# Attention and two feed-forward layers on one core: another list schedule behind the same instructions

## The chip, the core and the metric

The kernel runs on one core of a Trainium2 chip. Its time is device microseconds for one execution, and the smaller the better. The core's engines are named as in the profile: PE multiplies matrices, PEld loads its weights, DVE and POOL work on vectors, ACT evaluates functions, SP issues the transfers. Each engine takes its instructions in the order in which they were written into its own stream and waits on semaphores for the others.

## What is computed

```
scores = scale * q @ k.T                       # batch 4, 8 heads, 576 positions, 64 wide
masks  = local (0 <= i-j < 32) for heads 0..3, strided (i-j >= 0, same rest mod 32) for 4..7
x      = softmax(where(masks, scores, -1e9)) @ v      # -> 2304 tokens x 512
h  = x @ w_in                                  # 512 -> 2048
g  = (a0 + a1 h + a2 h^2 + a3 h^3) / (1 + |b0||h| + |b1|h^2 + 1e-6)
y  = g @ w_out                                 # 2048 -> 512
h  = y @ w_in2                                 # 512 -> 1024
s  = h * softmax(h)
out = ((s - mean) / sqrt(var + 1e-6) * g_ln) @ w_out2 # 1024 -> 512
```

## The kernel before

All large products are made of three float16 matmuls (high by high, high by low, low by high); attention stays in float32. Batch 0's attention is done first, in 12 units of one pair of heads and up to two key blocks each (`attn_scores2` ... `attn_xlo`). Of each unit PE makes the scores, DVE their maxima, ACT the exponentials, DVE the sums and reciprocals, POOL the normalised weights, PE their transposes (`MATMUL bank<-ident,p`), ACT copies these out (`q<-bank`), PE multiplies with v (`bank<-q,vl` or `bank<-q,vs`), and ACT and DVE write the high and low halves of x (`xs<-bank`). Beside it DVE converts the weights: `w_conv` puts a word together from two halves in three instructions of 128x1024 each (writing into tiles called `T`, `gtb`, or free places in `wi_h`, `wo_h`, `wo_l`, `ysb`), and `w_split` makes a high half on ACT and a low half on DVE (`wi_l<-...`).

Then 72 groups follow, 9 blocks of 256 tokens by 8 groups of 256 features. A group is 24 matmuls into one of two banks (`mm_h`, `bank<-xs,wi_h` and `wi_l`), an elementwise chain over ACT, POOL and DVE that ends with `q<-q,bank`, `bank<-q,bank` and `p<-p,ac,bank` on DVE and frees the bank, two halves of the result in a ring (`gtb`, or free weight places for the first 16 groups), and 24 more matmuls (`mm_y`, `banks<-gtb,wo_h`). Group n+2 needs the bank of group n. Below, "group n" counts from 0, and "the end of group n" is its last DVE instruction. Beside the groups run the attention of batches 1 to 3 on spare slots, the conversion of `w_out`, `w_in2` and `w_out2` (`w2_split` runs on POOL for its low halves, `wo_l<-ws,wo_h`), and the second layer, 18 tiles of 128 tokens (`mm_in2`: `banks<-wi_h,ysb`; a softmax and a norm on ACT and DVE in `ws`; transposes by DMA; `mm_out2`: `bank<-wo_h,T`).

What sets the order is the class `Order`. The program is recorded, not emitted. `record` (L156) notes each instruction's reads, writes and predecessors; `cost` (L201) gives each a planned duration; `run` (L237) makes a list schedule over all engines; `emit` (L334) writes the instructions out in that order, so that nearly every row of the profile bears line L341 and tiles must tell them apart. `run` first goes backwards once and gives every instruction a due time, then places them forward: on each engine, among those that can begin within `SLACK` (L110) of the earliest, the one with the earliest due time. A reader on another engine may begin after the writer's end, the writer's delay and a margin:

```
LAG = dict(PE=0.25, ACT=0.15, DVE=0.13, POOL=0.1, SP=0.0)
EARLY, PEARLY = 0.3, 1.5
o.ready = max(o.ready, end + (0.0 if o.eng == op.eng == "PE" else 0.06 if o.eng == op.eng
          else LAG[op.eng] + (PEARLY if o.eng == "PE" else EARLY)))
```

A matmul's planned duration is doubled while a count of recent matmul time (`heat`, `warm`, L307) is low, whatever the matmuls' type. Instructions marked `op.port` (POOL, and DVE instructions with two operands in SBUF or in its fast forms) are planned one after the other (`port`).

Of the kernel before, what the change touches and what calls it, by code (L numbers as in the profile page):

```python
# [106 lines left out]


BUSY = 1e9
SLACK = 0.2  # L110
RATE = 330e3


class Order:
# [86 lines left out]
    def cost(self, op):  # L201
        def size(x):
            n = 1
            for d in x.shape[1:]:
                n *= d
            return n

        ins = [(b, x) for b, x in op.ins if size(x) > 1]
        psum = any(b for b, _ in op.ins + op.outs)
        out = (op.outs or op.ins)[0][1]  # L210
        n = max([size(out)] + [size(x) for _, x in ins])
        op.port, op.land = False, 0.0
        if op.eng == "PE":
            f32 = op.ins[-1][1].dtype == F32
            op.t = max(0.03, size(out) / 2400 * ((3.6 if op.call == "transpose" or out.shape[0] > 64 else 1.8) if f32 else 1))
        elif op.eng == "ACT":
            op.t = 0.08 + n * 0.00088 + (0.05 if psum else 0) + (0.09 if "accum_out" in op.k else 0)
            op.t += 0.08 if n > 300 and hasattr(op.k.get("bias"), "shape") else 0
        elif op.eng == "DVE":
            sb = [x for b, x in ins if not b]  # L220
            two = op.call in ("scalar_tensor_tensor", "tensor_tensor")
            fast = not two and not psum and op.call == "tensor_scalar"
            op.t = 0.07 + n / (1900 if fast else 960) + (0.08 if "accum_out" in op.k else 0)
            op.t += 0.06 * sum(1 for b, x in op.ins if size(x) == 1)
            op.port = n >= 8 and (len(sb) >= 2 if two else fast)
        elif op.eng == "POOL":
            two = op.call == "tensor_tensor"
            h = two and out.dtype == F16
            op.t = 0.1 + n * (0.002 if h else 0.0022 if two else 0.00125 if op.call == "tensor_scalar" else 0.001)
            op.t += 0.1 if op.call == "tensor_scalar" and n < 32 else 0  # L230
            op.port = bool(ins)
        else:
            op.t = 0.06
            b = n * self.SIZE[out.dtype] * out.shape[0]
            op.land = b

    def run(self):  # L237
        ops = self.ops
        LAG = dict(PE=0.25, ACT=0.15, DVE=0.13, POOL=0.1, SP=0.0)
        EARLY, PEARLY = 0.3, 1.5  # L240

        after = 0.0
        for i, op in enumerate(ops):
            op.then = list(op.post)
            for v in op.values:
                v.__dict__.setdefault("users", []).append(i)
        for q in self.queues.values():
            for v, w in zip(q, q[len(q[0].homes):]):
                for j in v.users:
                    if j < w.users[0]:  # L250
                        ops[j].then.append(w.users[0])
        for op in reversed(ops):
            x = min([ops[j].due - (LAG[op.eng] + EARLY if ops[j].eng != op.eng else 0.0) for j in op.then], default=0.0)
            if op.eng == "PE":
                x = min(x, after)
            d = op.t
            if op.eng == "SP":
                d = 2.0 + op.land / 330e3
            op.due = x - d
            if op.eng == "PE":  # L260
                after = op.due
        free = {e: 0.0 for e in self.real}
        cells, port, dma = {}, 0.0, 0.0
        avail = {e: [] for e in self.real}
        need = [len(op.pre) for op in ops]
        for i, op in enumerate(ops):
            op.ready = 0.0
            if not need[i]:
                avail[op.eng].append(i)

        def begin(op):
            x = max(free[op.eng], op.ready)
            if op.port:
                x = max(x, port)
            for v in op.values:
                if v.home is None:
                    f = [max(cells.get(c, 0.0) for c in h) for h, _ in v.homes]
                    x = max(x, min(f)) if v.queue[0] is v else BUSY
            return x

        done, seq, heat, warm = 0, [], 0.0, False
        while done < len(ops):
            best = None
            for e, xs in avail.items():
                if not xs:
                    continue
                c = [(begin(ops[i]), ops[i].due, i) for i in xs]
                t = min(c)[0]
                if t == BUSY:
                    continue  # L290
                t, d, i = min((x for x in c if x[0] <= t + SLACK), key=lambda x: x[1:])
                if best is None or t < best[0]:
                    best = (t, i)
            assert best is not None, "no instruction can be placed"
            t, i = best
            op = ops[i]
            avail[op.eng].remove(i)
            for v in op.values:
                if v.home is None:
                    f = [(max(cells.get(c, 0.0) for c in h), j) for j, (h, _) in enumerate(v.homes)]  # L300
                    v.home = min(f)[1]
                    v.queue.pop(0)
                    for c in v.homes[v.home][0]:
                        cells[c] = BUSY
            d = op.t
            if op.eng == "PE":
                heat = min(3.4, max(0.0, heat - max(0.0, t - free["PE"])) + d)  # L307
                warm = heat > 3.3 or warm and heat > 1.5
                d = d if warm else 2 * d
            end = t + d  # L310
            free[op.eng] = end
            if op.port:
                port = end
            if op.eng == "SP":
                dma = max(dma, t + 0.5) + op.land / RATE
                end = dma + 1.6
            op.end = end
            for v in op.values:
                v.left -= 1
                v.end = max(getattr(v, "end", 0.0), end)  # L320
                if not v.left:
                    for c in v.homes[v.home][0]:
                        cells[c] = v.end + LAG[op.eng] + EARLY
            for j in op.post:
                o = ops[j]
                o.ready = max(o.ready, end + (0.0 if o.eng == op.eng == "PE" else 0.06 if o.eng == op.eng else LAG[op.eng] + (PEARLY if o.eng == "PE" else EARLY)))
                need[j] -= 1
                if not need[j]:
                    avail[o.eng].append(j)
            seq.append((t, i))  # L330
            done += 1
        return seq

    def emit(self, seq):  # L334
        def real(x):
# [994 lines left out]
```

## Time and profile before

| | |
|---|---|
| three runs | 770.37, 772.98, 773.19 us; median 772.98 |
| profiled execution | 773.43 us, of which the span from first to last instruction is 771.6 |
| PE busy | 712.6 us (92%), 5406 instructions |
| DVE busy | 592.0 us (77%), 1194 instructions |
| ACT, POOL busy | 481.8 us (62%), 328.6 us (43%) |
| mean granted clock of PE | 0.929 of full |
| chain that ended last | PE 71%, DVE 17%, DMA 4%, issue 4%, ACT 3% |

The profile's page gives one profiled execution. A view by stretches gives each engine's busy time and the granted clock; the timeline gives single instructions with the idle time before them and what ended it. Where PE is busy for the whole of a stretch at full clock, only fewer matmuls could shorten it; where it is not, the difference is what an order of instructions can win or lose.

### The profile page before, as it was taken

How to read it: one execution, taken by the hardware profiler on the slowest of the kernel's cores; microseconds unless marked ns; L12 is line 12 of the kernel's file. 1: busy time of each engine (PE TensorE's matmuls, PEld its weight loads, DVE VectorE, ACT ScalarE, POOL GpSimd, SP SyncE). 2: the span in 40 equal slices, each digit the busy share in tenths (PEclk: the TensorE clock that was granted, in tenths of full speed). 3: DMA queues.
4: the chain of work that ended last, by engine and by line, in shares of the span. 5: the costliest groups of instructions: out<-in, count | busy, mean ns of one | idle time of the engine just before them, and what ended most of it. 6: DMA issues, size and time to landing. Idle time of an engine off the chain costs nothing.

```text
span 771.6 us, 14358 instructions
## 1 busy us (share of the span) xinstructions
PE 712.6 (92%) x5406; PEld 540.0 (70%) x5406; DVE 592.0 (77%) x1194; ACT 481.8 (62%) x1143; POOL 328.6 (43%) x312
## 2 busy tenths in 40 slices
PE   3985667999998998999999999999999999999996
PEld 3863456888887887787777777777777777765442
DVE  6789999989999999798976677666666766744562
ACT  2685568678778867977766676455555646533342
POOL 3322234664667948465353435344444535320000
PEclk9555567999999999999999999999999999999999
DMA  9988701124414221123121020102201011012134
GB/s 272 320 209 218 197 1 33 34 97 142 123 57 140 60 70 34 34 63 61 28 47 42 2 42 1 42 1 43 42 1 42 10 33 42 1 42 55 41 82 96
DMA packets 68101, 55.98 MB, mean 73 GB/s; under 512 B 39616, under 2 KB 56000, under 8 KB 67520
## 3 DMA queue, kind: packets, MB, share of 16 engines
q1 hardware_dynamic: 68032, 55.07, 27.6%
q8 instruction: 42, 0.69, 0.4%
q14 instruction: 27, 0.22, 0.1%
HBM read 40.90 MB, written 4.72 MB: 59 GB/s over the span
## 4 chain that ended last, share of the span: by engine, by line
PE 71%; DVE 17%; DMA 4%; issue 4%; ACT 3%; SPq 0%; POOL 0%; ACTq 0%; DVEq 0%
PE bank L341 39%; PE banks L341 32%; DVE p L341 3%; DVE tiny L341 3%; DMA qkb<-in_qk_dram 2%; DVE T L341 2%; DVE gtb L341 2%; DMA vs<-in_v_dram 1%; DVE ws L341 1%; DVE bank L341 1%; DVE xs L341 1%; DVE q L341 1%; DVE wi_l L341 1%; ACT p L341 1%; DVE ysb L341 1%
## 5 line engine op out<-in xcount | busy, mean ns | idle before, releaser
L341 PE MATMUL bank<-xs,wi_h 128*128 128x256 f16 x1152 | 203.5, 281 | 13.4 <-DVE p L341 9.4
L341 PE MATMUL bank<-xs,wi_l 128*128 128x256 f16 x576 | 161.5, 280 | 2.3 <-DVE wi_l L341 2.3
L341 PE MATMUL banks<-gtb,wo_h 128*128 128x256 f16 x896 | 152.1, 273 | 0.1
L341 POOL TENSOR_SCALAR q<-A,aba 128x512 f32<-128x512 f32 x72 | 65.0, 902 | 181.4 <-ACT A L341 181.3
L341 PEld LDWEIGHTS <-wi_h 128*128 128x128 f16 x1152 | 115.7, 101 | 29.6 <-issue 13.4
L341 PEld LDWEIGHTS <-wo_h 128*128 128x128 f16 x1152 | 112.4, 98 | 21.9 <-issue 0.8
L341 PE MATMUL banks<-gtb,wo_l 128*128 128x256 f16 x448 | 122.0, 273 | 0.0
L341 DVE SCALAR_TENSOR_TENSOR p<-p,ac,bank 128x512 f32<-128x512 f32 x144 | 107.5, 747 | 4.7
L341 ACT ACTIVATE A<-bank,ih 128x512 f32<-128x512 f32 x72 | 49.4, 686 | 79.4 <-PE bank L341 79.1
L341 POOL TENSOR_TENSOR q<-q,A 128x512 f32<-128x512 f32 x72 | 91.6, 1272 | 5.5
L341 PE MATMUL banks<-wi_h,ysb 128*128 128x512 f16 x288 | 91.1, 379 | 0.0
L341 PE MATMUL bank<-wo_h,T 128*128 128x512 f16 x272 | 86.3, 383 | 3.0 <-DMA T<-ws 3.0
L341 DVE TENSOR_TENSOR p<-p,bank 128x512 f32<-128x512 f32 x72 | 49.1, 682 | 50.2 <-ACT p L341 49.7
L341 POOL TENSOR_TENSOR gtb<-p,gtb 128x512 f16<-128x512 f32 x56 | 73.5, 1315 | 25.2 <-ACT gtb L341 25.0
L341 PEld LDWEIGHTS <-T 128*128 128x128 f16 x408 | 40.1, 99 | 47.7 <-DMA T<-ws 4.0
L341 PEld LDWEIGHTS <-ysb 128*128 128x128 f16 x432 | 42.2, 98 | 44.0
L341 DVE SCALAR_TENSOR_TENSOR q<-q,bank 128x512 f32<-128x512 f32 x72 | 49.1, 682 | 24.6 <-ACT bank L341 18.7
L341 PEld LDWEIGHTS <-wi_l 128*128 128x128 f16 x576 | 58.1, 101 | 12.3 <-DVE wi_l L341 2.4
L341 POOL TENSOR_TENSOR e<-e,tiny 96x508 f32<-96x508 f32 (+3 forms) x36 | 35.6, 989 | 72.1 <-DVE tiny L341 32.3
L341 ACT ACTIVATE L<-q 128x512 f32<-128x512 f32 x72 | 45.3, 629 | 26.1 <-POOL q L341 26.1
L341 PEld LDWEIGHTS <-wo_l 128*128 128x128 f16 x576 | 56.5, 98 | 6.4
L341 ACT ACTIVATE e<-bank,tiny 96x127 f32<-96x127 f32 (+2 forms) x132 | 45.8, 356 | 20.4 <-DVE tiny L341 15.9
(257 smaller groups left out, 1435.2 us busy)
## 6 DMA issues: line engine op xcount, KB each, us to landing
qkb<-in_qk_dram SPq DMA_DIRECT2D x28, 304.0 KB, 4.5
out_dram<-ot SPq DMA_DIRECT2D x18, 256.0 KB, 2.4
wo_h<-in_w_out_dram SPq DMA_DIRECT2D x4, 1024.0 KB, 6.2
wo_l<-in_w_out_dram SPq DMA_DIRECT2D x4, 1024.0 KB, 7.1
vl<-in_v_dram SPq DMA_DIRECT2D x4, 768.0 KB, 4.2
wi_h<-in_w_in_dram SPq DMA_DIRECT2D x3, 1024.0 KB, 5.0
wi_l<-in_w_in_dram SPq DMA_DIRECT2D x3, 1024.0 KB, 5.6
wo_h<-in_w_in_dram SPq DMA_DIRECT2D x3, 1024.0 KB, 16.6
```

Of the source, the lines that this page charges most:

```text
L341: getattr(self.real[op.eng], op.call)(*[real(x) for x in op.a], **{k: real(x) for k, x in op.k.items()})
```

## The change

Only the planner is changed; every recorded instruction stays, and the number on each engine is the same (DVE 1176, PE 5039 matmuls, ACT 907, POOL 315). The planned durations of matmuls, small ACT instructions and transfers are set anew; a reader's margin falls from 0.3 to 0.1 and for PE from 1.5 to 0.5; a follower on the same engine now waits for the engine's delay (0.06 before); `SLACK` falls from 0.2 to 0.05. A forward placement is followed by a backward one from the planned end, which gives new due times, in four turns, and the order with the earliest planned end is kept.

```diff
-SLACK = 0.2
-RATE = 330e3
@@ cost
         if op.eng == "PE":
             f32 = op.ins[-1][1].dtype == F32
-            op.t = max(0.03, size(out) / 2400 * ((3.6 if op.call == "transpose" or out.shape[0] > 64 else 1.8) if f32 else 1))
+            op.t = size(out) / 2400 + 0.0025
+            if op.call == "transpose":
+                op.t = 2 * op.t
+            elif f32:
+                op.t = 2 * size(out) / 2400 + 0.055 if out.shape[0] == 64 else 4 * op.t + 0.03
...
+            op.t = max(op.t, 0.11)
...
+    LAG = dict(PE=0.21, ACT=0.14, DVE=0.12, POOL=0.09, SP=0.0)
+    EARLY, PEARLY, SLACK = 0.1, 0.5, 0.05
+
+    def lag(self, op, to, early=1.0):
+        if op.eng == to.eng:
+            return 0.0 if op.eng == "PE" else self.LAG[op.eng]
+        return self.LAG[op.eng] + (0.07 if to.eng == "POOL" else 0.0) + early * (self.PEARLY if to.eng == "PE" else self.EARLY)
@@ run
-        LAG = dict(PE=0.25, ACT=0.15, DVE=0.13, POOL=0.1, SP=0.0)
-        EARLY, PEARLY = 0.3, 1.5
...
+        self.first_due()
+        best = None
+        for k in range(self.TURNS):
+            seq, end, homes = self.forward()
+            if best is None or end < best[0]:
+                best = (end, seq, homes)
+            if k < self.TURNS - 1:
+                self.backward(end)
...
+    TURNS = 4
...
+    def backward(self, T):
...
+        for _ in ops:
+            best = None
+            for e, xs in avail.items():
+                if xs:
+                    c = [(max(free[e], ops[i].ready, port if ops[i].port else 0.0), -ops[i].end, -i) for i in xs]
+                    t = min(c)[0]
+                    t, d, i = min((x for x in c if x[0] <= t + self.SLACK), key=lambda x: x[1:])
+                    if best is None or t < best[0]:
+                        best = (t, -i)
...
+            op.due = -end
+            for j in op.before:
+                o = ops[j]
+                o.ready = max(o.ready, end + self.lag(o, op, 0.5))
...
@@ forward (the second half of run before)
-                o.ready = max(o.ready, end + (0.0 if o.eng == op.eng == "PE" else 0.06 if o.eng == op.eng else LAG[op.eng] + (PEARLY if o.eng == "PE" else EARLY)))
+                o.ready = max(o.ready, end + self.lag(op, o))
```

Three places of the order follow. The first is DVE in batch 0's attention, at the low half of x of unit 6 (`xs_107` and `xs_108`, 128x8x14); the tiles `wo_l`, `wo_h` and `wi_l` beside it belong to the conversion of `w_in`. Before:

```order
L341 TENSOR_SCALAR wo_l<-wo_l 128x1024
L341 SCALAR_TENSOR_TENSOR wo_l<-wo_l 128x1024 x2
L341 TENSOR_REDUCE tiny<-bank_87 108x2
L341 SCALAR_TENSOR_TENSOR wi_l<-wo_h,scl_wi,wi_h 128x4x256
L341 TENSOR_REDUCE tiny<-smb_129 126x4
L341 RECIPROCAL tiny<-tiny 126x4
L341 SCALAR_TENSOR_TENSOR wi_l<-T_102,scl_wi,wi_h 128x4x256
L341 SCALAR_TENSOR_TENSOR xs_107<-bank_88,xsc_134,xs_107 128x8x14
L341 SCALAR_TENSOR_TENSOR xs_108<-bank_88,xsc_134,xs_108 128x8x14
```

With the change:

```order
L409 TENSOR_REDUCE tiny<-g_t 128x1
L409 TENSOR_SCALAR wo_h<-wo_l 128x1024
L409 TENSOR_REDUCE tiny<-bank_86 108x2
L409 SCALAR_TENSOR_TENSOR xs_107<-bank_88,xsc_134,xs_107 128x8x14
L409 SCALAR_TENSOR_TENSOR xs_108<-bank_88,xsc_134,xs_108 128x8x14
L409 SCALAR_TENSOR_TENSOR wo_h<-wo_l,wo_h 128x1024
L409 TENSOR_REDUCE tiny<-bank_87 108x2
L409 SCALAR_TENSOR_TENSOR wo_h<-wo_l,wo_h 128x1024
```

Eight instructions that stood ahead of the low half of unit 6 now stand behind it: two `wo_h<-wo_l,wo_h`, the three of `wo_l<-wo_l`, the two `wi_l` and one maximum.

The second place is POOL where it makes the low halves of the last weight, `wo_l<-ws`, between the groups' own instructions (`q`, `gtb`) and the normalisation of batch 2's attention (`e`). Before:

```order
L341 TENSOR_TENSOR q_97<-q_97,A_99 128x512
L341 TENSOR_TENSOR gtb<-p_94,gtb 128x2x256
L341 TENSOR_TENSOR e_92<-e_92,tiny 108x2x108
L341 TENSOR_TENSOR wo_l<-ws_104,wo_h 128x512 x4
L341 TENSOR_SCALAR q_98<-A_99,aba 128x512
L341 TENSOR_TENSOR q_98<-q_98,A_99 128x512
```

With the change:

```order
L409 TENSOR_TENSOR gtb<-p_96,gtb 128x2x256
L409 TENSOR_TENSOR wo_l<-ws_104,wo_h 128x512 x2
L409 TENSOR_SCALAR q_98<-A_99,aba 128x512
L409 TENSOR_TENSOR q_98<-q_98,A_99 128x512
L409 TENSOR_TENSOR e_92<-e_92,tiny 108x2x108
L409 TENSOR_TENSOR wo_l<-ws_104,wo_h 128x512 x2
L409 TENSOR_TENSOR gtb<-p_94,gtb 128x2x256
```

The four in a row are now two pairs. On DVE, the two small instructions `ac_154<-ih_152,tiny` that stood before the `q` of group 26 now stand before that of group 23, three groups ahead of these pairs.

The third place is DVE between the `q` of group 19 and that of group 20 (`q_98` and `q_97` here); `ws_104` and `T_102` belong to the conversion of `w_out2`. Before:

```order
L341 SCALAR_TENSOR_TENSOR q_98<-q_98,bank_87 128x512
L341 SCALAR_TENSOR_TENSOR bank_87<-q_98,bank_87 128x512
L341 SCALAR_TENSOR_TENSOR p_95<-p_95,ac_144,bank_87 128x512
L341 TENSOR_REDUCE tiny<-bank_89 96x2
L341 SCALAR_TENSOR_TENSOR xs_107<-bank_88,xsc_151,xs_107 128x128
L341 SCALAR_TENSOR_TENSOR xs_108<-bank_88,xsc_151,xs_108 128x64
L341 TENSOR_REDUCE tiny<-bank_89 96x2
L341 SCALAR_TENSOR_TENSOR T_102<-wo_l,T_102 128x1024
L341 SCALAR_TENSOR_TENSOR q_97<-q_97,bank_86 128x512
```

With the change:

```order
L409 SCALAR_TENSOR_TENSOR q_98<-q_98,bank_87 128x512
L409 SCALAR_TENSOR_TENSOR bank_87<-q_98,bank_87 128x512
L409 SCALAR_TENSOR_TENSOR p_95<-p_95,ac_144,bank_87 128x512
L409 TENSOR_REDUCE tiny<-smb_129 96x4
L409 RECIPROCAL tiny<-tiny 96x4
L409 SCALAR_TENSOR_TENSOR xs_108<-bank_88,xsc_151,xs_108 128x192
L409 TENSOR_SCALAR ws_104<-wo_h 128x1024
L409 TENSOR_SCALAR qkb_127<-qkb_127 128x576
L409 SCALAR_TENSOR_TENSOR ws_104<-wo_h,ws_104 128x1024
L409 SCALAR_TENSOR_TENSOR q_97<-q_97,bank_86 128x512
```

By the `q` of group 20 five more instructions have been issued than before: the second `T<-wo_l,T`, `ws<-wo_h`, `ws<-wo_h,ws`, one `qkb<-qkb` and the `xs` of 128x192. On PE, by the first `mm_h` matmul of group 22, ten 512-wide matmuls of the second layer's tile 0 (`banks<-wi_h,ysb` and `wi_l`) and four transposes of attention have been issued more. From group 30 on the groups' matmuls stand at the same place on PE.

## Rows read from the trace of the kernel before

**Rows 1.** Busy time by stretches: us, PE, PEld, DVE, ACT, POOL busy (instructions), clock, DMA, GB/s.
```profile
20.00:60.00 40.00, 34.74 (x187) 30.12 (x188) 33.69 (x71) 30.10 (x104) 11.12 (x9) 0.50 0.90 248
60.00:130.00 70.00, 43.02 (x238) 31.75 (x238) 68.36 (x138) 43.76 (x105) 22.73 (x15) 0.56 0.48 124
130.00:207.00 77.00, 76.12 (x720) 66.35 (x719) 71.81 (x157) 58.91 (x163) 45.59 (x46) 1.00 0.29 90
207.00:264.00 57.00, 52.82 (x482) 44.96 (x482) 54.53 (x113) 45.44 (x115) 41.21 (x35) 1.00 0.28 90
264.00:298.00 34.00, 33.49 (x304) 28.70 (x301) 32.78 (x54) 23.90 (x56) 21.36 (x23) 1.00 0.17 55
298.00:321.00 23.00, 20.89 (x170) 16.15 (x168) 20.80 (x44) 18.65 (x58) 14.27 (x15) 0.93 0.12 29
321.00:747.00 426.00, 425.74 (x3202) 307.89 (x3200) 288.81 (x579) 247.71 (x520) 165.56 (x150) 1.00 0.17 35
747.00:772.00 25.00, 17.98 (x76) 7.34 (x74) 8.75 (x19) 7.47 (x14) 0.00 (x0) 0.93 0.34 84
```

**Rows 2.** Timeline near 300 us: start, duration, engine, instruction [idle before, releaser].
```profile
300.10 5.40 DVE L341 TENSOR_SCALAR ac<-ih,tiny 128x8 f32<-128x8 f32 x2
300.22 4.50 POOL L341 TENSOR_TENSOR wo_l<-ws,wo_h 128x512 f16<-128x512 f32 x4
...
307.65 0.38 PE L341 MATMUL bank<-xs,wi_h 128*128 128x256 f16 x2 [1.77 <-DVE p L341]
```

**Rows 3.** Timeline of DVE, a small fast instruction with no POOL run beside it.
```profile
294.60 0.36 DVE L341 TENSOR_SCALAR ac<-tiny 128x8 f32<-128x8 f32 x2
```

**Rows 4.** Timeline of DVE near 260 us: what now stands ahead of group 20's q.
```profile
260.73 0.67 DVE L341 SCALAR_TENSOR_TENSOR q<-q,bank 128x512 f32<-128x512 f32 x1
...
264.13 0.42 DVE L341 SCALAR_TENSOR_TENSOR xs<-bank,xsc,xs 128x192 f16<-128x192 f32 x1 [0.35 <-ACT xs L341]
...
265.12 2.00 DVE L341 SCALAR_TENSOR_TENSOR T<-wo_l,T 128x1024 int32<-128x1024 int32 x1
267.04 0.68 DVE L341 TENSOR_SCALAR ws<-wo_h 128x1024 int32<-128x1024 int32 x1
...
271.13 1.90 DVE L341 SCALAR_TENSOR_TENSOR ws<-wo_h,ws 128x1024 int32<-128x1024 int32 x1
...
310.34 0.45 DVE L341 TENSOR_SCALAR qkb<-qkb 128x576 f32<-128x576 f32 x1
```

**Rows 5.** Timeline of PE near 260 us: four transposes, two 512-wide matmuls, group 22's first.
```profile
259.83 0.58 PE L341 MATMUL bank<-ident,e 96*127 96x96 f32 x4
...
262.33 0.38 PE L341 MATMUL banks<-wi_h,ysb 128*128 128x512 f16 x1
262.54 0.38 PE L341 MATMUL banks<-wi_l,ysb 128*128 128x512 f16 x1
...
263.78 0.38 PE L341 MATMUL bank<-xs,wi_h 128*128 128x256 f16 x2
```

**Rows 6.** Timeline of DVE, 50 to 61 us: conversion and the low half of unit 6.
```profile
50.18 1.21 DVE L341 SCALAR_TENSOR_TENSOR wo_h<-wo_l,wo_h 128x1024 int32<-128x1024 int32 x1
...
54.96 2.48 DVE L341 SCALAR_TENSOR_TENSOR wo_l<-wo_l 128x1024 int32<-128x1024 int32 x2
...
57.66 1.28 DVE L341 SCALAR_TENSOR_TENSOR wi_l<-wo_h,scl_wi,wi_h 128x1024 f16<-128x1024 f32 x1
...
60.37 0.57 DVE L341 SCALAR_TENSOR_TENSOR xs<-bank,xsc,xs 128x112 f16<-128x112 f32 x2
```

**Rows 7.** Timeline of PE and ACT, 44 to 57 us: waits inside the attention chain.
```profile
45.78 0.91 PE L341 MATMUL bank<-q,vl 127*64 127x96 f32 x8 [1.85 <-ACT q L341]
56.11 1.12 PE L341 MATMUL bank<-q,vs 126*64 126x126 f32 x8 [1.10 <-ACT q L341]
...
44.20 1.06 ACT L341 ACTIVATE wi_h<-ysb 128x1024 f16<-128x1024 f32 x1 [2.02 <-DVE ysb L341]
```

**Rows 8.** Timeline of DVE near the end: the low half of tile 16.
```profile
752.10 1.23 DVE L341 TENSOR_TENSOR ws<-ws 128x1024 f16<-128x1024 f32 x1
```

More of the change, by code (lines that the diff above doesn't have):

```diff
@@ L232, in cost @@
         else:
-            op.t = 0.06
-            b = n * self.SIZE[out.dtype] * out.shape[0]
-            op.land = b
+            op.t = 0.55
+            rows, run = min(x.shape[0] for _, x in op.ins + op.outs), min(x.ap[-1][1] for _, x in op.ins + op.outs)
+            op.land = n * self.SIZE[out.dtype] * out.shape[0] / (170e3 if op.call != "dma_start" else 240e3 if rows == 64 else 300e3 if run <= 128 else 375e3)
+    LAG = dict(PE=0.21, ACT=0.14, DVE=0.12, POOL=0.09, SP=0.0)
[4 more added lines that the diff above has]
+        return self.LAG[op.eng] + (0.07 if to.eng == "POOL" else 0.0) + early * (self.PEARLY if to.eng == "PE" else self.EARLY)
     def run(self):
         ops = self.ops
-        LAG = dict(PE=0.25, ACT=0.15, DVE=0.13, POOL=0.1, SP=0.0)
-        EARLY, PEARLY = 0.3, 1.5
-        after = 0.0
         for i, op in enumerate(ops):
@@ L251, in run @@
                         ops[j].then.append(w.users[0])
-        for op in reversed(ops):
-            x = min([ops[j].due - (LAG[op.eng] + EARLY if ops[j].eng != op.eng else 0.0) for j in op.then], default=0.0)
+        for op in ops:
+            op.before = []
+        for i, op in enumerate(ops):
+            for j in op.then:
+                ops[j].before.append(i)
+        self.first_due()
[6 more added lines that the diff above has]
+                self.backward(end)
@@ L254, in run, with first_due @@
+        _, seq, homes = best
+        for v, h in homes:
+            v.home = h
+        return seq
+    TURNS = 4
+    def first_due(self):
+        after = 0.0
+        for op in reversed(self.ops):
+            x = min([self.ops[j].due - self.lag(op, self.ops[j], 0.5) for j in op.then], default=0.0)
             if op.eng == "PE":
                 x = min(x, after)
[L256 to L259, printed above, removed]
+            op.due = x - (2.6 + op.land if op.eng == "SP" else op.t)
@@ L260, in run @@
             if op.eng == "PE":
                 after = op.due
+    def backward(self, T):
+        ops = self.ops
+        free, port, dma = {e: 0.0 for e in self.real}, 0.0, 0.0
+        avail = {e: [] for e in self.real}
+        need = [len(op.then) for op in ops]
+        for i, op in enumerate(ops):
+            op.ready = 0.0
+            if not need[i]:
+                avail[op.eng].append(i)
+        for _ in ops:
[7 more added lines that the diff above has]
+                        best = (t, -i)
+            t, i = best
+            op = ops[i]
+            avail[op.eng].remove(i)
+            free[op.eng] = end = t + op.t
+            if op.port:
+                port = end
+            if op.eng == "SP":
+                dma = max(dma, t) + op.land
+                end = dma + 2.6
+            op.due = -end
+            for j in op.before:
+                o = ops[j]
+                o.ready = max(o.ready, end + self.lag(o, op, 0.5))
+                need[j] -= 1
+                if not need[j]:
+                    avail[o.eng].append(j)
@@ L262, in run, with forward @@
+    def forward(self):
+        ops = self.ops
         free = {e: 0.0 for e in self.real}
@@ L265, in run @@
         need = [len(op.pre) for op in ops]
+        queue = {k: list(q) for k, q in self.queues.items()}
+        for k, q in self.queues.items():
+            for v in q:
+                v.home, v.left, v.end, v.queue = None, len(v.users), 0.0, queue[k]
         for i, op in enumerate(ops):
@@ L279, in begin @@
             return x
-        done, seq, heat, warm = 0, [], 0.0, False
-        while done < len(ops):
+        seq, heat, warm = [], 0.0, False
+        while len(seq) < len(ops):
             best = None
@@ L290, in run @@
                     continue
-                t, d, i = min((x for x in c if x[0] <= t + SLACK), key=lambda x: x[1:])
+                t, d, i = min((x for x in c if x[0] <= t + self.SLACK), key=lambda x: x[1:])
                 if best is None or t < best[0]:
@@ L314, in run @@
             if op.eng == "SP":
-                dma = max(dma, t + 0.5) + op.land / RATE
+                dma = max(dma, t + 1.0) + op.land
                 end = dma + 1.6
@@ L319, in run @@
                 v.left -= 1
-                v.end = max(getattr(v, "end", 0.0), end)
+                v.end = max(v.end, end)
                 if not v.left:
                     for c in v.homes[v.home][0]:
-                        cells[c] = v.end + LAG[op.eng] + EARLY
+                        cells[c] = v.end + self.LAG[op.eng] + self.EARLY
             for j in op.post:
                 o = ops[j]
-                o.ready = max(o.ready, end + (0.0 if o.eng == op.eng == "PE" else 0.06 if o.eng == op.eng else LAG[op.eng] + (PEARLY if o.eng == "PE" else EARLY)))
+                o.ready = max(o.ready, end + self.lag(op, o))
                 need[j] -= 1
@@ L330, in run @@
             seq.append((t, i))
-            done += 1
-        return seq
+        return seq, max(op.end for op in ops), [(v, v.home) for q in self.queues.values() for v in q]
     def emit(self, seq):
```

## The prediction

> **What bounds the kernel now.** The first view is the busy time by stretches, since an average over the whole span hides that the stretches have different limits [rows 1]. From 321 to 747 us PE is busy for 425.74 of 426 us at full clock. No order of the same matmuls is shorter there, and PE's order of the groups is the same from group 30 on, so 426 of the 772 us are out of reach. What can change lies ahead of 321 us and in the last 25. From 60 to 130 us DVE is the limit (68.36 of 70), with PE at clock 0.56. From 130 to 207 PE is nearly full (76.12 of 77) and DVE has 5.2 us free. From 207 to 264 neither is full: PE idles 4.18, DVE 2.5. From 298 to 321 PE idles 2.11 at a clock of 0.93; a mean of 0.93 over two levels, 1.2 and 2.4 GHz, is 3.2 of 23 us at the lower one, which loses 1.6 us of work.
>
> The second view, the timeline, tells why. At 300.10 two tiny DVE instructions take 5.40 us while POOL makes four large ones in a row in 4.50 [rows 2]; the same kind of pair with POOL quiet takes 0.36 [rows 3]. DVE stood still for 5.0 us, the next group's last DVE instruction came late, and PE waited 1.77 for it at 307.65. That is the largest single stall in the middle of the program.
>
> **The change, term by term.** The instructions stay; only their order and so the waits change. The sum is made against the profiled execution, 773.4 us, which lies 0.4 above the median of the runs.
>
> *The collision at 300 us goes.* The two `ac` instructions now stand three groups ahead of POOL's four, and the four are two pairs. What it cost PE is the idle time and the lower clock of that stretch, 2.11 + 1.6 = 3.7. I take all of it: -3.7. The other bound is 0: each pair still lasts 4.50 / 2 = 2.25, and another short DVE instruction beside each could be held twice, 4.5 in all, nearly the 5.0 of before. I stay near the first, because PE's wait was 1.77 after a hold of 5.0, so a hold of 2.25 alone would be hidden.
>
> On this the row and a rule differ. The row shows that DVE did not get in between POOL's four: it waited for all of them [rows 2]. The Trainium skill, page "SBUF — State Buffer", section "SBUF: two separate sides", calls the port that DVE and POOL share an exclusive lock, held for a whole instruction; by it a DVE instruction should wait for one POOL instruction, an estimate of 4.50 / 4 = 1.1, where the trace has 5.0, so they don't agree in size. By the page even a pair would cost 1.1 at most and the term stays -3.7; by the row it may be 2.25.
>
> *Group 20's end comes later.* DVE, ahead of the `q` of group 20, now also issues a `T<-wo_l,T` (2.00), `ws<-wo_h` (0.68), `ws<-wo_h,ws` (1.90), one `qkb` (0.45) and an `xs` (0.42): 5.45 [rows 4]. Group 22's matmuls, at 263.78 before, wait for the bank that this group's last instruction frees. PE for its part has ten 512-wide matmuls more to do by then, 10 x 0.21 by the distance of two starts, and four transposes (0.58), 2.7 in all [rows 5]. The difference, 2.8, is new idle time on PE: +2.8. Bounds: +0.3, if DVE's 2.5 idle of 207 to 264 [rows 1] takes up half of it, and +5.45, if PE's extra matmuls themselves wait. I take the middle value since DVE's idle there is scattered between its waits for PE.
>
> *What it gives back.* Work done early is not to be done later: from 264 to 298 DVE has 32.78 of 34 and PE idles 0.51 [rows 1]. That goes: -0.5 (bounds 0 and -0.5).
>
> *Batch 0's attention.* The low half of unit 6, `xs` at 60.37, stands ahead of two `wo_h` (1.21 each), three `wo_l` (0.68 by the like row of `ws`, and 2.48 for two), two `wi_l` (1.28 each) and a small maximum: 8.1 with the maximum left out, some 8.3 with it [rows 4, 6]. DVE will issue it 8.3 us of its own work earlier, and can wait there with the conversions queued behind it. How much of this is waiting depends on PE and ACT. PE waited 1.85 and 1.10 for copies by ACT in this chain, and ACT 2.02 for DVE's `ysb` [rows 7]. If the new deadlines put the copies ahead of conversions, those two PE waits, 2.95, go, and 5.3 of DVE waiting is left. DVE's free 5.2 us of 130 to 207 [rows 1] cover just that, and PE's 4.18 idle of 207 to 264 lies behind as a second cover. So I count 0. Without the cover it costs up to 8.3. The other bound is a gain: DVE is idle 6.3 of 40 us from 20 to 60 [rows 1], and a better order could save all of it, -6.3.
>
> *The tail.* The low half of tile 16 (1.23) [rows 8] and tile 17's product have changed places on DVE; both are needed before the last matmuls. 0, bounds -1.2 and +1.2.
>
> *The margins.* A reader may now be placed 0.2 us, on PE 1.0 us, closer behind its writer. Such a reader is at the head of its queue and holds what follows. No row shows the new waits. The nearest are PE's waits of 1.77 and 1.85 [rows 2, 7]; three of them make +5.4. The lower bound is that PE's 4.18 idle of 207 to 264 [rows 1] goes, -4.2. With PE full in most stretches after 130 us there is little idle time for a tighter order to win, and about as much to lose: 0.
>
> **Sum.** -3.7 + 2.8 - 0.5 + 0 + 0 + 0 = -1.4, so 773.4 - 1.4 = 772.0 against the profiled execution, and with the 0.4 between it and the median **771.6 us**. A measurement of this kernel can tell about 0.5%, 3.9 us, from no change, so this is a forecast of no change that can be told: under 769.1 is faster, over 776.9 slower. The case's own range, from half of the margins' gain, -2.1, to the collision's term at 0, is 769 to 776 (rounded outward).
>
> **Rivals.**
>
> *The waits of the middle go instead of moving.* The deadlines from the second pass also put the second layer's first tile earlier on DVE; if that smooths the stretch, the +2.8 doesn't come and PE's 4.18 and 0.51 of idle time go too: -3.7 - 4.7 = -8.4, so 764.6. For it: those idle microseconds are there, and DVE is not full beside them. Against it: the five instructions ahead of group 20. Chance 0.29.
>
> *The clock comes up sooner.* From 20 to 60 us PE is busy 34.74 of 40 at clock 0.50, the 1.2 GHz level, and from 60 to 130 at 0.56 [rows 1]. If a denser attention let the higher level begin there, DVE would be the limit: its 6.3 idle of 20 to 60 and 1.6 of 60 to 130 go, -1.4 - 6.3 - 1.6 = -9.3, so 763.7. The Trainium skill, page "TensorE: Matmul & The Clock Gate", section "What's actually happening", has the throttled clock as the default, and activity as what releases it. The trace of this case agrees after 130 us, and speaks against it from 20 to 60: 87% busy, and still the lower level. So it gets 0.07.
>
> *The early low half holds DVE (slower).* The place is the `xs` of unit 6 and those of the units behind it, in front of conversions that the first groups need. If PE and ACT are not sooner and the cover of 5.2 isn't reached, since DVE's idle there belongs to waits for PE, the whole 8.3 comes through: -1.4 + 8.3 = +6.9, so 779.9. It decides once DVE comes to 130 us more than 5.2 late. For it: DVE's 68.36 of 70 from 60 to 130, where nothing is absorbed. Against it: the two PE waits that may go. Chance 0.27.
>
> *The order only moves waits about.* The collision comes back elsewhere; 773.0. It belongs to the forecast's side of the bound and is in its chance.
>
> **How the numbers follow.** Forecast with "only moves" 0.37, faster 0.29 + 0.07 = 0.36, slower 0.27. The range goes down to 762, just under both fast rivals, and up to 781, over the slow one; it leaves the cases where two mishaps or two gains add up.
>
> **What would show it.** In the stretch 298 to 321 PE full and clock 1.00, the pair of `ac` at about 0.4 us: the first term right. A PE wait of about 3 us before group 22's first matmul (near 262): the second. DVE's busy time in 20 to 60 under 33 us, with waits for ACT's `xs` before its own: the head's price begins; the start of the solid stretch (321 before) then tells what was left of it. PE at 1.00 before 110 us would be the clock rival. The forecast is wrong if the solid stretch begins more than 4 us earlier or later than at 321, or if there is idle time in PE after it.

## The result and the profile after

The changed kernel takes 775.49 us (median of nine runs, 773.75 to 778.9), the kernel before 770.7 us in nine runs (769.6 to 774.64): 1.0062 times the time before, interval 1.0038 to 1.0085. It is slower by 0.6%, just over what a measurement can tell. The forecast was 771.6 us and no change.

Busy time by stretches of the changed kernel (us, PE, PEld, DVE, ACT, POOL busy, clock, DMA, GB/s), in the stretches of [rows 1]:

```profile
20.00:60.00 40.00, 33.16 (x206) 27.54 (x204) 32.34 (x72) 32.07 (x113) 11.25 (x9) 0.63 1.00 270
60.00:130.00 70.00, 38.00 (x240) 29.12 (x241) 69.97 (x143) 43.87 (x96) 22.46 (x17) 0.67 0.43 111
130.00:207.00 77.00, 75.37 (x701) 65.04 (x701) 72.69 (x153) 56.89 (x162) 43.89 (x43) 0.99 0.31 92
207.00:264.00 57.00, 54.26 (x489) 45.69 (x488) 54.64 (x111) 44.18 (x111) 38.69 (x34) 1.00 0.34 107
264.00:298.00 34.00, 29.03 (x250) 24.69 (x249) 28.13 (x50) 20.71 (x52) 18.70 (x22) 0.90 0.11 34
298.00:321.00 23.00, 22.70 (x205) 18.32 (x202) 21.19 (x49) 21.35 (x62) 14.87 (x16) 1.00 0.18 41
321.00:747.00 426.00, 422.62 (x3188) 306.69 (x3186) 284.74 (x572) 247.13 (x513) 163.29 (x151) 1.00 0.16 33
```

Three stretches differ in kind. 298 to 321 is full and at full clock: the collision of [rows 2] is gone, as forecast. 264 to 298, nearly full before, has 5.0 us of idle PE and a clock of 0.90. And the long stretch from 321 to 747, which had 0.26 us of idle time, has 3.4. The starts of groups on PE, read from the timelines, divide the difference of the two spans, 777.1 - 771.6 = 5.5:

| first matmul of | before | after | later by |
|---|---|---|---|
| group 20 | 248.25 | 244.09 | -4.2 |
| group 30 | 330.68 | 332.12 | +1.4 |
| (end) | 771.6 | 777.1 | +5.5 |

```profile
248.25 0.38 PE L341 MATMUL bank<-xs,wi_h 128*128 128x256 f16 x2 [1.58 <-DVE p L341]
330.68 0.38 PE L341 MATMUL bank<-xs,wi_h 128*128 128x256 f16 x2
```

```profile
244.09 0.38 PE L409 MATMUL bank<-xs,wi_h 128*128 128x256 f16 x2 [1.21 <-DVE p L409]
332.12 0.38 PE L409 MATMUL bank<-xs,wi_h 128*128 128x256 f16 x2
```

So in this pair of traces the front wins 4.2 us, the ten groups in the middle lose 5.6, and the part whose order of matmuls is the same loses 4.0 (445.0 us from group 30 to the end, 441.0 before).

**The middle.** Timelines of DVE, POOL and PE of the changed kernel (start, duration, engine, instruction, idle before and its releaser):

```profile
261.29 2.33 DVE L409 TENSOR_SCALAR qkb<-qkb 128x576 f32<-128x576 f32 x1 [0.23 <-DMA qkb<-in_qk_dram]
263.54 3.98 DVE L409 SCALAR_TENSOR_TENSOR ws<-wo_h,ws 128x1024 int32<-128x1024 int32 x1
267.44 0.68 DVE L409 SCALAR_TENSOR_TENSOR q<-q,bank 128x512 f32<-128x512 f32 x1
```

```profile
263.05 1.04 POOL L409 TENSOR_SCALAR q<-A,aba 128x512 f32<-128x512 f32 x1
264.07 1.15 POOL L409 TENSOR_TENSOR gtb<-p,gtb 128x512 f16<-128x512 f32 x1
265.18 1.25 POOL L409 TENSOR_TENSOR q<-q,A 128x512 f32<-128x512 f32 x1
```

```profile
269.68 0.59 PE L409 MATMUL bank<-xs,wi_h 128*128 128x256 f16 x2 [4.97 <-DVE p L409]
```

The `ws<-wo_h,ws` began at 263.54, while POOL was in the first of these three. They are the end of a run, that is of instructions without idle time between them, which goes back to 255.96. The last of them ended at 266.43, and DVE's ended 1.1 us later, about the time that such an instruction takes alone (1.22, experiment 3). It was held to the end of POOL's run, as the `ac` pair was at 300 us before. The `qkb<-qkb` ahead of it was held too (2.33, alone 0.45), but ended at 263.62, while that run went on. The `q` of group 20 stood behind both, and PE waited 4.97 us for group 22's first matmul. The clock then stood at its lower level (1.2 GHz) from 268.2 to 275.0.

**The full stretch.** What PE waited for from 331 to 760 us, before and after (us in total, times, longest):

```profile
PE bank L341 <- DMA T<-ws: 3.0, 2, 2.2
PE bank L341 <- DVE tiny L341: 0.3, 1, 0.3
```

```profile
PE banks L409 <- ACT ysb L409: 3.4, 6, 0.6
PE bank L409 <- DMA T<-ws: 1.3, 1, 1.3
```

The six waits for `ysb` are new. One of them, on PE and on ACT:

```profile
525.76 0.38 PE L409 MATMUL banks<-gtb,wo_h 128*128 128x256 f16 x2
526.70 0.27 PE L409 MATMUL banks<-gtb,wo_l 128*128 128x256 f16 x1 [0.56 <-ACT ysb L409]
```

```profile
526.17 0.47 ACT L409 ACTIVATE ysb<-banks,cy 128x256 f16<-128x256 f32 x1 [0.67 <-PE banks L409]
```

These are the last matmuls of a block of 256 tokens, whose product fills a tile of two banks in four parts. ACT's first copy reads the first part, whose bank is complete six matmuls before the block's end. The planner follows each bank by itself. PE's delay and the margin were 0.25 + 0.3 = 0.55 us, just longer than the 0.53 planned from the end of the first bank to the start of the block's last matmul (five of 256 / 2400); now they are 0.21 + 0.1 = 0.31. So the planner may now place this copy ahead of the last `wo_l`, which writes the other bank. When the instructions are written out in that order, waits are set for the tile as a whole: the copy waits for the `wo_h` in front of it (it begins as that ends), and the `wo_l` waits for the copy. Counted in the order of emission, the copy stands ahead of the last matmul in seven of nine blocks now, and in none before. Five of the six places behind 331 us move all that follows by 0.72 to 0.73 us each.

### The profile page after: what moved, and what is told of

It is laid out like the page before. It is cut to its first block, busy times and chain, and to the rows that moved or that the text cites. A ratio compares the mean times of both kernels' runs of the same rounds, so it can differ in the third digit from the quotient of the medians.

```text
span 777.1 us, 14389 instructions
## 1 busy us (share of the span) xinstructions
PE 705.2 (91%) x5406; PEld 533.2 (69%) x5406; DVE 586.7 (75%) x1194; ACT 481.9 (62%) x1143; POOL 319.7 (41%) x312
## 4 chain that ended last, share of the span: by engine, by line
PE 75%; DVE 16%; ACT 4%; DMA 3%; issue 2%; SPq 0%; ACTq 0%; DVEq 0%
PE bank L409 40%; PE banks L409 34%; DVE tiny L409 3%; DVE T L409 2%; DVE p L409 2%; DMA wi_h<-in_w_in_dram 1%; DVE gtb L409 1%; DVE wi_l L409 1%; DMA qkb<-in_qk_dram 1%; DVE bank L409 1%; DVE ws L409 1%; DVE q L409 1%; ACT p L409 1%; DVE wo_h L409 1%; ACT e L409 1%
## 5 line engine op out<-in xcount | busy, mean ns | idle before, releaser
L409 PE MATMUL bank<-xs,wi_h 128*128 128x256 f16 x1152 | 200.9, 279 | 13.5 <-DVE p L409 10.7
L409 POOL TENSOR_SCALAR q<-A,aba 128x512 f32<-128x512 f32 x72 | 60.9, 846 | 159.5 <-ACT A L409 159.1
L409 POOL TENSOR_TENSOR gtb<-p,gtb 128x512 f16<-128x512 f32 x56 | 66.8, 1194 | 71.0 <-ACT gtb L409 71.0
L409 ACT ACTIVATE gtb<-p 128x512 f16<-128x512 f32 x56 | 35.4, 632 | 51.0 <-DVE p L409 50.8
L409 ACT ACTIVATE e<-bank,tiny 96x127 f32<-96x127 f32 (+2 forms) x132 | 46.2, 358 | 26.6 <-DVE tiny L409 24.3
```

The costliest lines, as they stand in the source:

```text
L409: getattr(self.real[op.eng], op.call)(*[real(x) for x in op.a], **{k: real(x) for k, x in op.k.items()})
```

## Experiments

Where an experiment edits an order, the instructions are written out again so that every engine keeps its own sequence but for what is named, and all dependences are kept. Each was compared with the kernel before, run on the same chip.

**1 and 2: the copies, taken out and put in.** Only the emission differs, every engine's sequence is the same.

```diff
+ # the changed kernel: every block's last eight matmuls (w, PE) ahead of its copies (u, not PE)
+ edges.update((w[-1 - k], j) for k in range(8) for j in u if self.ops[j].eng != "PE")
```

> The changed kernel with the same order on every engine; only the emission of the copies of the first product's result (ysb, ACT) is put behind the last matmul of the two-bank tile, so that the last wo_l or wo_h matmuls no longer wait for a copy. Theory (the six waits of 0.56 us between 380 and 707 us, 0.72 to 0.73 each in the distance to before, are made by the interleaving alone): 6 x 0.73 = 4.4 us less than the changed kernel, so about 771.1 us, no different from the kernel before (770.7), and no wait for ysb after 331 us. Rival (PE would be held there anyway, by ACT's copies being late or by the elementwise chain): 775 to 776, and another wait in the same places.

```diff
+ # the kernel before: in six blocks the first copy ahead of the last wo_l
+ edges.update(((3904, 3844), (4743, 4680), (5396, 5352), (6038, 5989), (6674, 6630), (7148, 7130)))
```

> The kernel before with the same order on every engine; in six blocks of tokens (the fourth to the ninth) the first copy of the result is emitted ahead of the block's last wo_l matmul, as in the changed kernel. Theory: six new waits of about 0.56 us, 6 x 0.72 = 4.3 us more, about 775.0 us against 770.7. Rival (the rest of the changed order makes PE wait there): within 0.5 us of the kernel before.

Without the waits the changed kernel takes 771.41 us (ratio to before 0.9986, 0.9973 to 1.0); with them the kernel before takes 777.55 us against 772.67 (1.0053, 1.0033 to 1.0073). The first is 4.1 us less than the changed kernel by the medians and 5.9 by the ratios, the second 4.1 us more than the kernel before by its ratio and 4.9 by the medians. The traces, from group 30 to the end, leave the front out: 440.7 us for the first against 445.0, and 444.7 for the second against 441.0. That is what the theory asked for, in both directions. PE's row for 321 to 747 of the first, and the only line of PE's waits from 331 to 760 us in the second:

```profile
321.00:747.00 426.00, 426.00 (x3188) 306.86 (x3186) 284.83 (x576) 245.11 (x508) 159.41 (x147) 1.00 0.17 35
```

```profile
PE banks L342 <- ACT ysb L342: 3.4, 6, 0.6
```

The same sequence on each engine is 0.5% faster or slower by the interleaving alone. This is shown, not argued.

**3: the middle.**

```diff
  # the changed kernel, DVE
- ws<-wo_h   qkb<-qkb   ws<-wo_h,ws      (ahead of the q of group 20)
+ the same three behind the last p of groups 20 and 21
```

> The changed kernel; on DVE ws<-wo_h, qkb<-qkb and ws<-wo_h,ws (7.5 us of DVE between 259.84 and 267.44 in its trace) are moved behind the last p of groups 20 and 21. Theory (these three, slowed by POOL, are what held group 20's end and with it PE for 4.97 us, and brought the lower clock of 268.2 to 275.0, 3.4 us): 3 to 8 us less, about 769 us, with the wait ahead of group 22 under 1 us and clock 1.00 from 264 to 298. Rival (the early work is given back later, so the wait only moves on to groups 22 to 24): 774 to 776.

769.72 us, 0.9965 (0.9948 to 0.9982): 5.8 us less than the changed kernel by the medians, 7.5 by the ratios, and in the traces groups 20 to 30 take 82.0 us instead of 88.0. With no run of POOL beside them the three take what such instructions take alone:

```profile
263.96 0.69 DVE L410 TENSOR_SCALAR ws<-wo_h 128x1024 int32<-128x1024 int32 x1
264.56 0.45 DVE L410 TENSOR_SCALAR qkb<-qkb 128x576 f32<-128x576 f32 x1
264.93 1.22 DVE L410 SCALAR_TENSOR_TENSOR ws<-wo_h,ws 128x1024 int32<-128x1024 int32 x1
```

2.4 us in sum against 7.5. PE has no wait ahead of group 22; two of 0.65 and 0.47 us are left ahead of group 23's (270.7 and 272.2). The rival, that the wait only moves, falls but for these. PE's early matmuls of the second layer stay in place in this run, so they were not what cost. The move takes both the three's own 2.4 us and the 5.1 that POOL added from ahead of the `q`; no run takes away POOL's part alone. By the lengths, an estimate, it is enough: 5.1 us less would have covered the wait of 4.97. In its new place the hold goes the other way: POOL's `q<-A,aba` at 266.27 takes 3.23 us (0.76 at 259.47) beside three more of DVE's conversions, up to 269.03.

**4: the old collision, alone.**

```diff
  # the kernel before, DVE
- ac<-ih,tiny x2     (beside POOL's four wo_l<-ws,wo_h)
+ the same two behind ac<-tiny x2, a group earlier
```

> The kernel before; on DVE the two ac instructions that took 5.40 us at 300.10 stand right behind their sister pair at 294.60, one group earlier. Theory (the collision with POOL's four instructions costs PE 3.7 us): about 767 us against 770.7, clock 1.00 from 298 to 321. Rival (POOL's own q stands behind the four as well, so DVE's next group waits for it): at most 1 us less, with DVE waiting for ACT or POOL at 305.

770.09 us, 0.9961 (0.9946 to 0.9976), by which it is 3.0 us less. POOL's four are as long as in [rows 2], and the pair is short:

```profile
293.84 0.72 DVE L342 TENSOR_SCALAR ac<-ih,tiny 128x8 f32<-128x8 f32 x2
```

```profile
299.19 4.51 POOL L342 TENSOR_TENSOR wo_l<-ws,wo_h 128x512 f16<-128x512 f32 x4
```

The stretch from 298 to 321 is at clock 1.00 with 22.61 us of busy PE. The rival, that POOL's own `q` behind the four would hold the group, falls.

**5: both edits at the changed kernel.**

> The changed kernel with both edits at once: copies of the first product's result emitted behind the last matmul of their tile, and the three DVE instructions moved behind the last p of groups 20 and 21. Theory (two separate causes, which add up): 769.7 of the moved one less 4.3 for six waits of 0.72 us, about 765.4 us, 0.7 to 0.9% under the kernel before in the same call. Rival (they share a cause, or what is won in the middle is lost behind): 768 to 770.

764.36 us, 0.9905 (0.9882 to 0.9929). The two causes add up: the ratios of experiments 1 and 3, 0.0076 and 0.0097 under the changed kernel's 1.0062, ask for 0.9889, inside the interval.

**6: a planner that knows the tile.**

```diff
  if (op.outs if w else op.ins)[-1][0]:
      ...
+     if len(x.value.homes[0][0]) == 2:
+         m = (1 << 1024) - 1
```

> The changed kernel whose planner is told that a tile of two banks is waited for as a whole; nothing else. The plan has no copy ahead of the last matmul of its block any more, and the order of all engines is planned anew. Theory: no wait for ysb behind 331 us, 4.3 us less from there; ahead of 331 us the order is another throw, within 4 us either way, so about 771 us (767 to 775). Rival (the planner only shifts the same waits to other tiles): 775 or more, with waits of PE for ACT of about 0.5 us at the ends of blocks.

765.36 us, 0.9915 (0.9892 to 0.9938), and no wait for `ysb` after 331 us. The waits went as the theory said; the time lies under its range of 767 to 775. In this kernel the third turn has the earliest planned end (750.1 us) and is kept, so its order is another one throughout: group 30 begins at 326.82 instead of 332.12, and from there to the end it takes 437.9 us instead of 445.0. What of this is due to the tile and what to the new order can't be told apart.

**7 and 10: margins and durations, one at a time.**

```diff
  # the kernel before
- EARLY, PEARLY = 0.3, 1.5        SLACK = 0.2
+ EARLY, PEARLY = 0.1, 0.5        SLACK = 0.05
```

> The kernel before with the new margins alone (0.1 and 0.5 instead of 0.3 and 1.5, and 0.05 instead of 0.2 for SLACK); durations and delays as before. In its order four of the nine blocks have a copy ahead of their last matmuls (none in the kernel before, seven in the changed one). Theory (the margins make these waits): four new waits for ysb, 4 x 0.72 = 2.9 us, so about 774 us against 771, give or take 3 for the order ahead of 331 us. Rival (margins are harmless, the new durations did it): within 1.5 us of the kernel before, no waits for ysb behind 331 us.

```diff
  # the changed kernel
- EARLY, PEARLY, SLACK = 0.1, 0.5, 0.05
+ EARLY, PEARLY, SLACK = 0.3, 1.5, 0.2
```

> The changed kernel with the old margins (0.3, 1.5, 0.2); new durations, delays and passes. Three of the nine blocks have a copy ahead of their last matmuls. Theory (the smaller margins are what costs, the new durations are worth something): three waits, 2.2 us, and an order ahead of 331 us at least as good as before, 767 to 773 us. Rival (the new durations and delays bring the loss): 775 or more.

The new margins alone take 788.35 us, 1.021 (1.0183 to 1.0237), much worse than either theory; the new durations with the old margins take 770.39 us, 0.9971 (0.9954 to 0.9989). In the kernel with the new margins alone the four waits are there (2.3 us in sum), and its longest wait of PE is once more behind a DVE instruction beside a run of POOL:

```profile
266.24 6.24 DVE L341 SCALAR_TENSOR_TENSOR ws<-wo_h,ws 128x1024 int32<-128x1024 int32 x1
```

```profile
266.16 1.03 POOL L341 TENSOR_TENSOR e<-e,tiny 96x508 f32<-96x508 f32 x1 [2.72 <-DVE tiny L341]
267.15 1.15 POOL L341 TENSOR_TENSOR gtb<-p,gtb 128x512 f16<-128x512 f32 x1
268.29 0.77 POOL L341 TENSOR_SCALAR q<-A,aba 128x512 f32<-128x512 f32 x1
269.02 1.15 POOL L341 TENSOR_TENSOR gtb<-p,gtb 128x512 f16<-128x512 f32 x1
270.13 1.26 POOL L341 TENSOR_TENSOR q<-q,A 128x512 f32<-128x512 f32 x1
```

```profile
277.15 0.59 PE L341 MATMUL bank<-xs,wi_h 128*128 128x256 f16 x2 [8.41 <-DVE p L341]
```

Five POOL instructions end at 271.39 and DVE's at 272.48: a 1.2 us instruction held for 5 us, and PE idle for 8.41. A second meeting stands behind PE's wait of 5.74 us at 235.98: `ih<-inv_wi,xp`, 128x8, takes 4.06 us from 228.40. By group starts this trace is 1.9 us later than the kernel before at group 20, loses 5.6 from there to group 30 and 6.2 behind it, so how much of the loss is due to the two meetings stays open. That margins as such cost 16 us can't be concluded; they let such meetings come about.

With the old margins two waits for `ysb` are left behind 331 us, 1.1 us in sum. So the waits are not the margins' alone: with the new delay the sum is 0.21 + 0.3 = 0.51 us, still under 0.53. This kernel isn't the changed one with other margins and nothing else, either: in it the third turn is planned to end first and is kept, so its order comes from the backward placement too.

**8, 11 and 12: the later turns.** The changed kernel keeps the order of its first turn, whose due times come from the same kind of first backward walk as before. Its four turns are planned to end at 747.3, 747.9, 750.7 and 748.4 us, so the backward placement changes nothing in the emitted program.

```diff
- if best is None or end < best[0]:
+ if k == 1:                     # 2 and 3 in the other two
      best = (end, seq, homes)
```

> The changed kernel made to take the order of its second turn, the first one whose due times come from the backward placement; the changed kernel itself keeps the order of its first turn, which is planned to end 0.6 us earlier. Theory (the backward due times change little that matters): the waits for ysb are there as well (six blocks from the fourth on), 775 us, give or take 3. Rival (the backward due times are worth something that the plan doesn't see): 771 us or less.

> The changed kernel made to take the order of its third turn, which is planned to end 3.4 us later than the first. Theory (the backward due times are good on the chip, whatever the plan says; five waits for ysb from the fifth block on, 3.6 us): 762 to 768 us. Rival (the planned end tells which order is faster, and the second turn was luck): 775.5 + 3.4 = 779 us.

> The changed kernel made to take the order of its fourth turn, planned to end 1.2 us later than the first. Theory (backward due times are good on the chip; waits for ysb in the third to the ninth block, 7 x 0.72 = 5 us): 763 to 769 us. Rival (the planned end tells): 775.5 + 1.2 = 776.7 us.

764.23 us (0.99, 0.9874 to 0.9925), 774.68 us (1.0024, 1.0007 to 1.0042) and 776.88 us (1.0058, 1.0038 to 1.0079). So the second turn's order is 11 us faster than the first's, and the other two are not. The difference lies ahead of group 30, which begins at 318.27, 330.09 and 331.65 us in the second, third and fourth turn and at 332.12 in the first; from there to the end they take 442.8 to 445.1. The theory that backward due times are good on the chip falls with the last two. The rival's numbers, 779 and 776.7, fit only the last, and the fourth turn, planned 0.5 us behind the second, is 12.7 us slower. Ends that the planner puts within 3.4 us of each other lie 12.7 us apart on the chip, in another order.

**9: the best.** The second turn's order, with the copies of blocks four to nine behind their last matmuls.

> The order of the second turn, as in the run before, with the copies of the first product's result emitted behind the last matmul of their tile in blocks four to nine; the order on every engine is that of the second turn. Theory (the six waits are apart from what the due times win): 764.2 - 6 x 0.72 = 759.9 us, 1.5% under the kernel before. Rival (the waits hide another limit in this order): 763 to 764.

759.49 us, 0.983 (0.9807 to 0.9854), as expected, and faster than both kernels. Groups 20 to 30 take 77.7 us, 88.0 in the changed kernel. The stretch from 207 to 264, and PE's waits from 331 to 760 us:

```profile
207.00:264.00 57.00, 56.22 (x513) 47.61 (x511) 53.12 (x114) 46.25 (x116) 45.42 (x36) 1.00 0.34 110
```

```profile
PE bank L410 <- DMA T<-ws: 1.6, 2, 1.0
PE bank L410 <- ACT ot L410: 0.4, 1, 0.4
```

## Why the prediction was wrong

**The step that failed** is the first: "No order of the same matmuls is shorter there, and PE's order of the groups is the same from group 30 on, so 426 of the 772 us are out of reach." Out of reach for a gain, yes; a full engine can still lose. PE's sequence is the same there, but what a matmul waits for depends on where the other engines' instructions stand in the emission. With it fell the term of the margins: taken as 0, the new waits measured +4.1 (experiments 1 and 2). The smaller delay of PE has a part in them too (experiment 10). The term's upper bound, +5.4 for three new waits, held, though for other waits: six of 0.56 us. The prediction had named idle time of PE behind 321 us as a sign that it is wrong, and that sign came.

**Group 20's end** was the right place and mechanism, mis-sized. The prediction added 5.45 us of DVE work ahead of the `q`, from durations of rows; in the changed kernel the same five instructions took 9.2 (1.21, 0.42, 1.22, 2.33, 3.98), since two of them met runs of POOL. The wait was 4.97, not 2.8, and 6.8 us at half clock add 3.4, 8.4 in all. Less the 3.0 of the collision below, that is 5.4 for the middle, where the traces have 5.6. The prediction had seen exactly this at 300 us and priced it as gone; it didn't look at what POOL does beside the instructions that move.

**The collision at 300 us**: -3.7, measured -3.0 alone (experiment 4). Right in itself, though the changed kernel builds the same thing anew at 261 to 267 us, so over the whole kernel it was moved and not won. That is the last rival, "the collision comes back elsewhere", at more than twice the price of the old place.

**On the rule**: POOL's runs held DVE for three, four and five instructions (3.98 us, [rows 2], 6.24 us), so for these the row was the one to go by. The Trainium skill, page "SBUF — State Buffer", section "SBUF: two separate sides", has the shared port locked for one whole instruction; these three don't agree. But the trace of the kernel before has a case that does:

```profile
257.98 2.83 DVE L341 SCALAR_TENSOR_TENSOR T<-wo_l,T 128x1024 int32<-128x1024 int32 x1
```

```profile
257.60 2.12 POOL L341 TENSOR_TENSOR wi_l<-ws,wi_h 128x1024 f16<-128x1024 f32 x1
259.69 2.14 POOL L341 TENSOR_TENSOR gtb<-p,gtb 128x512 f16<-128x512 f32 x1
```

Here DVE ended 1.1 us after the first of POOL's two, and POOL's second took 2.14 us instead of 1.15, though no idle time stands between them: DVE got in after one instruction. The `qkb` of the changed kernel got in as well, after two. Whether DVE is held for one instruction of a run or for all of it is not explained by any run here. Nor was POOL quite quiet beside the pair of [rows 3]: it ran instructions of 0.32 and 0.74 us from 294.28 and 294.70.

**Batch 0's attention** was counted as 0 and won about 4 in the profiled pair. The low half of unit 6 ran at 52.80 instead of 60.37 with no wait noted before it, so the slower rival with its 8.3 didn't occur, though its sign (DVE under 33 us of busy time from 20 to 60: 32.34) did. What in the front's order wins, no run separates. How much the front wins in general is uncertain: in four traces with the same order up to there (the changed kernel, experiments 1, 3 and 5) group 20 begins at 244.09, 239.72, 240.96 and 238.93; in three of before's order (the kernel before, 2 and 4) at 248.25, 248.01 and 247.16. The changed kernel's own trace is the slowest of its four, and the kernel before's the slowest of its three. The medians of all runs, 4.8 us apart, ask for a front of 4.8 - 5.6 - 4.0 = -4.8, inside the stated bound of -6.3; the means of these four and three starts, 240.9 and 247.8, make it -6.9, outside.

**The clock rival**, given 0.07: the granted clock did rise, to 0.63 and 0.67 in the first two stretches, against 0.50 and 0.56. But the order of the kernel before shows 0.67 and 0.63 in experiment 2, and 0.59 and 0.64 in experiment 4, so this rise is no mark of the change. Nor did it bring the time: in experiment 2 group 20 begins only 0.24 us earlier than in the kernel before. In both DVE is busy for nearly all of the 70 us from 60 to 130 (67.69 and 68.36). The two stretches in experiment 2, as in [rows 1]:

```profile
20.00:60.00 40.00, 28.83 (x184) 24.82 (x184) 33.97 (x71) 30.25 (x106) 11.72 (x9) 0.67 0.90 249
60.00:130.00 70.00, 41.19 (x245) 30.66 (x245) 67.69 (x136) 42.84 (x102) 22.37 (x15) 0.63 0.47 123
```

**What it gives back** (-0.5) and **the tail** (0): the 264 to 298 stretch went the other way for the reason above. In the tail nothing is lost: from the last matmul that reads `ysb` (747.37 before, 752.82 after) to the end of the span it is 24.3 us in both.

**The second pass**: the prediction took "new deadlines" as a working part of the change, in its term on attention and in the first rival. They are not in the emitted order at all. That this part does nothing should have been a rival of its own.

The range, 762 to 781, held the time, in part by luck: the middle came out 7.0 us above its terms (+5.6 for -1.4) and the part behind it 4.0 above, and the front's 4.2 below took some of that back. The chance of slower, 0.27, was put on the wrong mechanism.

## What to carry to other kernels

An engine that is full can't gain from another order, but it can lose by it: look at what its instructions will wait for, and check that the planner's unit of dependence (here a bank) is the one for which waits are set (a tile). Before costing DVE instructions that move, read what POOL does beside their new place; a run of POOL without a gap can hold a short one to the run's end, and with it all that stands behind it. And where orders differ by less in the plan than the plan is wrong by, run several on the chip and keep the fastest: here that was worth 11 us, more than the whole change.

## What was not expected of the hardware

A DVE instruction of 1.2 us took 6.24 us beside five POOL instructions in a row, and 3.98 us beside three, while another of this form (`T<-wo_l,T`, 2.83 us) was let in after one. The hold can grow with POOL's run, and the length of the run doesn't tell whether it will.

The same order of instructions on each engine reached group 20 between 238.93 and 244.09 us in four traces (two of them, experiments 1 and 5, without a wait of PE for a copy at 186 us). Most of this was there by the first matmul of group 0, at 53.49 to 58.06 us; from there to group 20 they took 185.4 to 186.0. From group 30 to the end two kernels with one order and one emission (the kernel before and experiment 4) took 441.0 and 441.1. In these traces nearly all of the spread between kernels of one order lies in the front.
